# One load queue, other places for transposes and statistics, and a split last tile in an attention-and-GLU kernel

## The chip, the cores and the metric

The kernel runs on one core of one Trainium2 chip. The metric is the device time of one execution in microseconds (us). A profile of the same execution has a span, from the first to the last instruction, that is 1.7 to 1.8 us shorter than the timed figure. TensorE is PE in the profile (its weight loads PEld), VectorE is DVE, ScalarE is ACT, GpSimd is POOL, SyncE is SP.

## The reference, cut to what matters

```python
xn = _layernorm(x)                    # x: 2048 x 512, bf16
s  = _A_ref(xn, wqkv, wo)             # 32 heads of 16, each position looks at 8 places, 2 apart
g  = _silu(_B_ref(xn, w_gate, w_up, w_down))   # (gelu(xn w_gate) * (xn w_up)) w_down, inner width 1792
return x + s * g
```

## The kernel before

The 2048 rows are 16 tiles of 128, four tiles to a chunk of 512. For each tile VectorE computes mean and variance (`moments`), GpSimd turns the variance into a reciprocal root, VectorE normalizes, TensorE transposes and ScalarE copies the transposed tile out of PSUM. Then TensorE runs all projections. The parts that the change and the argument touch:

```python
    for t in range(TPQ):                                   # TPQ = 4
        load_x(t, queue=nc.scalar if t % 2 else nc.sync)   # 128 KB each
    for i in range(3):
        load_w(wqkv_sb, A_wqkv, i * D, (i + 1) * D)        # q, k, v thirds, 512 KB each
    load_x(TPQ, TPQ)                                       # tiles 4 to 7
    # [cut: the other weights and tiles, all on nc.sync]

    def moments(t):
        nc.vector.bn_stats(out=stats[:, t, :], in_=x_sb[:, t, :])
        nc.vector.bn_aggr(out=mv[:, t, :], in_=stats[:, t, :])
        nc.gpsimd.tensor_scalar(
            out=rstd[:, t, :], in0=mv[:, t, 1:2], scalar1=EPS, scalar2=None, op0=ALU.add
        )
        nc.gpsimd.tensor_tensor(out=rstd[:, t, :], in0=rstd[:, t, :], in1=mhalf[:], op=ALU.pow)

    # [cut] schedule of side work: at((stage, chunk, step), function, arguments)
    for i in range(TPQ):
        at(("qkv", 0, i), normalize, TPQ + i)
        at(("qkv", 0, 4 + i), moments, 2 * TPQ + i)
        at(("glu", 0, i), transpose, TPQ + i)
        at(("glu", 0, 8 + i), normalize, 2 * TPQ + i)
        at(("qkv", 1, 1 + 3 * i), transpose, 2 * TPQ + i)
        at(("glu", 0, 8 + i), moments, 3 * TPQ + i)

    # [cut] the start
    warm_up(10, TQ)                 # ten matmuls of 512 columns on zeros
    moments(0); moments(1); normalize(0); transpose(0); normalize(1)
    warm_up(2, P); transpose(1); warm_up(2, P)
    moments(2); moments(3); normalize(2); normalize(3)
    # [cut: moments of tiles 4 to 7]
    for hh in range(2):             # first for tiles 0, 1, then for tiles 2, 3
        for fo in range(2 * NC):    # eight groups (4 of q, 4 of k) of four 256-column matmuls
            qkv(0, fo, hh * HT * P, HT * P)
            if hh == 0 and fo in (4, 7):
                transpose(HT + fo // 6)       # tiles 2 and 3
```

The end of a tile is `down`: 14 matmuls into y, Silu on ScalarE (`sl`), four matmuls into s, then on VectorE m = s * sl and o_t = m + x, and a store of o_t.

The names in the profile: tr and xnT are a transposed tile before and after its copy out of PSUM (the memory that TensorE writes to), qkv_ps the projections, g_ps and u_ps the two products of the GLU (`ge` and `u` once ScalarE has them, h their product), pk the products of q and k, L_ps the logits, E their Exp, pv the products of E and v, o_ps the attention output. A step is the third number of the schedule and counts from 0.

The softmax here doesn't subtract the row's maximum and nothing guards it: scores larger than these inputs give would overflow.

Of the kernel before, what the change touches and what calls it, by code (L numbers as in the profile page):

```python
# [8 lines left out]
ALU = mybir.AluOpType  # L9
AF = mybir.ActivationFunctionType  # L10
BF16 = mybir.dt.bfloat16
F32 = mybir.dt.float32

P = 128
# [7 lines left out]
TQ = 512  # L22
# [6 lines left out]
def kernel(  # L29
# [13 lines left out]
    nc = tc.nc  # L43
    B, S, D = A_x.shape
    DF = B_w_gate.shape[1]
    NT, NC, NF, NJ = S // P, D // P, DF // P, S // TQ
    TPQ = TQ // P
    SV = PAD + S
    x2d, out2d = A_x[0], out[0]
# [3 lines left out]
    def pool(name, bufs, **kw):  # L53
        return ctx.enter_context(tc.tile_pool(name=name, bufs=bufs, **kw))
# [10 lines left out]
    op = pool("op", 1)  # L65
    sm = pool("sm", 3)
    sm2 = pool("sm2", 2)
    sm4 = pool("sm4", 4)
    dram = pool("dram", 1, space=bass.MemoryType.DRAM)
    mm = pool("mm", 5, space=bass.MemoryType.PSUM)  # L70
# [3 lines left out]
    x_sb = big.tile([P, NT, D], BF16, name="x_sb")  # L74
# [4 lines left out]
    wo_sb = wts.tile([P, NC, D], BF16, name="wo_sb")  # L79
    vT = dram.tile([D, SV], BF16, name="vT")  # L80

    def load_x(t, n=1, queue=nc.sync):
        queue.dma_start(
            out=x_sb[:, t : t + n, :],
            in_=x2d[t * P : (t + n) * P, :].rearrange("(t p) d -> p t d", p=P),
        )
# [4 lines left out]
        )  # L91

    for t in range(TPQ):
        load_x(t, queue=nc.scalar if t % 2 else nc.sync)
    for i in range(3):
        load_w(wqkv_sb, A_wqkv, i * D, (i + 1) * D)
    load_x(TPQ, TPQ)
    for i, (lo, hi) in enumerate(((0, DF // 2), (DF // 2, DF))):
        load_w(wg_sb, B_w_gate, lo, hi)
        load_w(wu_sb, B_w_up, lo, hi)  # L100
        load_x((2 + i) * TPQ, TPQ)

    def load_late_weights():
# [15 lines left out]
        out=vT.rearrange("(k p) n -> p k n", p=P)[:, :, 0:PAD],  # L119
        in_=warm[:, 0 : NC * PAD].rearrange("p (k n) -> p k n", k=NC),  # L120
# [48 lines left out]
    def moments(t):  # L169
        nc.vector.bn_stats(out=stats[:, t, :], in_=x_sb[:, t, :])  # L170
        nc.vector.bn_aggr(out=mv[:, t, :], in_=stats[:, t, :])
        nc.gpsimd.tensor_scalar(
            out=rstd[:, t, :], in0=mv[:, t, 1:2], scalar1=EPS, scalar2=None, op0=ALU.add
        )
        nc.gpsimd.tensor_tensor(out=rstd[:, t, :], in0=rstd[:, t, :], in1=mhalf[:], op=ALU.pow)  # L175
# [10 lines left out]
    def transpose(t):  # L186
        xn = xns[t]
        tr = mm.tile([P, NC * P], BF16, name="tr", tag="mm")
        for c in range(NC):
            nc.tensor.transpose(tr[:, c * P : (c + 1) * P], xn[:, c * P : (c + 1) * P], ident[:])  # L190
        j, i = divmod(t, TPQ)
        if i == 0:
            xnT[j] = xtp.tile([P, NC, TQ], BF16, name="xnT")
        nc.scalar.activation(  # L194
            out=xnT[j][:, :, i * P : (i + 1) * P],
            in_=tr[:].rearrange("p (c n) -> p c n", c=NC),
            func=AF.Copy,
        )

    def warm_up(n, cols):  # L200

        ps = mm.tile([P, TQ], F32, name="warm_ps", tag="mm")
        for _ in range(n):
            nc.tensor.matmul(
                ps[:, 0:cols], lhsT=warm[:, 0:P], rhs=warm[:, 0:cols], start=True, stop=True
            )
# [11 lines left out]
    st = [dict(pk={}, pv={}) for _ in range(NJ)]  # L218

    def qkv(j, fo, i0=0, n=TQ):  # L220
        which, c = divmod(fo, NC)
        if fo == 0 and i0 == 0:
            st[j]["q"] = qp.tile([P, NC, TQ], BF16, name="q_sb")
        ps = mm.tile([P, n], F32, name="qkv_ps", tag="mm")
        project(ps, wqkv_sb, fo * P, j, i0, n)
        if which == 0:
            nc.scalar.activation(out=st[j]["q"][:, c, i0 : i0 + n], in_=ps[:], func=AF.Copy)  # L227
        elif which == 1:
            lo = PAD + j * TQ + i0
            nc.scalar.activation(out=k_sb[:, c, lo : lo + n], in_=ps[:], func=AF.Copy)  # L230
        else:
            vst = sm4.tile([P, TQ], BF16, name="vst")
            nc.scalar.activation(out=vst[:], in_=ps[:], func=AF.Copy)  # L233
            lo = PAD + j * TQ
            nc.sync.dma_start(out=vT[c * P : (c + 1) * P, lo : lo + TQ], in_=vst[:])
# [121 lines left out]
    def down(j, tt):  # L357
        y = mm.tile([P, D], F32, name="y_ps", tag="mm")
        for fc in range(NF):
            nc.tensor.matmul(  # L360
                y[:],
                lhsT=st[j][fc][:, tt * P : (tt + 1) * P],
                rhs=wd_sb[:, fc, :],
                start=(fc == 0),
                stop=(fc == NF - 1),
            )
        sl = sm2.tile([P, D], BF16, name="sl")
        nc.scalar.activation(out=sl[:], in_=y[:], func=AF.Silu)  # L368
        s = mm.tile([P, D], F32, name="s_ps", tag="mm")
        for g in range(NC):  # L370
            nc.tensor.matmul(  # L371
                s[:],
                lhsT=st[j]["oT"][:, g, tt * P : (tt + 1) * P],
                rhs=wo_sb[:, g, :],
                start=(g == 0),
                stop=(g == NC - 1),
            )
        t = j * TPQ + tt
        m = sm2.tile([P, D], BF16, name="m")
        nc.vector.tensor_tensor(out=m[:], in0=s[:], in1=sl[:], op=ALU.mult)  # L380
        o_t = sm4.tile([P, D], BF16, name="o_t")
        nc.vector.tensor_tensor(out=o_t[:], in0=m[:], in1=x_sb[:, t, :], op=ALU.add)
        nc.sync.dma_start(out=out2d[t * P : (t + 1) * P, :], in_=o_t[:])


    side = {}
# [1 line left out]
    def at(key, fn, *args):  # L388
        side.setdefault(key, []).append((fn, args))
# [4 lines left out]

    for i in range(TPQ):
        at(("qkv", 0, i), normalize, TPQ + i)
        at(("qkv", 0, 4 + i), moments, 2 * TPQ + i)
        at(("glu", 0, i), transpose, TPQ + i)
        at(("glu", 0, 8 + i), normalize, 2 * TPQ + i)
        at(("qkv", 1, 1 + 3 * i), transpose, 2 * TPQ + i)  # L400
        at(("glu", 0, 8 + i), moments, 3 * TPQ + i)
        at(("qkv", 2, 2 * i), normalize, 3 * TPQ + i)
        at(("qkv", 2, 3 + 2 * i), transpose, 3 * TPQ + i)

# [28 lines left out]


    HT = TPQ // 2
    warm_up(10, TQ)
    moments(0)
    moments(1)
    normalize(0)
# [12 lines left out]
    for hh in range(2):  # L452
        for fo in range(2 * NC):
            qkv(0, fo, hh * HT * P, HT * P)
            if hh == 0 and fo in (4, 7):
                transpose(HT + fo // 6)
    for i in range(NC):
        run("qkv", 0, i)
        run("qkv", 0, NC + i)
# [3 lines left out]
    for j in range(NJ):  # L463
        for fc in range(NF):
            run("glu", j, fc)
            glu(j, fc)
        if j + 1 < NJ:
            for i in range(12):
                run("qkv", j + 1, i)
                qkv(j + 1, i)  # L470
        for tt in range(TPQ):
            run("down", j, tt)
            down(j, tt)
# [28 lines left out]
```

## Time and profile before

| | before |
|---|---|
| timed, first three runs | 236.25 us (236.22 to 236.42) |
| span of the profiled run | 234.4 us |
| first projection starts | 7.54 us |
| second half of the first projections starts | 12.38 us |
| last matmuls (s_ps) start | 229.31 us |

Timeline lines read: start in us, duration in us, engine, line, operation, output<-inputs, shapes, count; in brackets, how long the engine had been idle and what released it. Lines of a group of matmuls start at the first and end at the last one. The main readings are in the prediction. Two lines of the timeline of the kernel before are added here, because the argument comes back to them: the wait of VectorE for the first x tile, and a ScalarE operation in step 8 of the first GLU.

```profile
3.20 0.69 DVE L170 BATCH_NORM_STATS2 stats<-x_sb 128x6 f32<-128x512 bf16 x1 [1.97 <-DMA x_sb<-in_A_x_dram]
...
36.32 0.60 ACT L352 ACTIVATE u<-u_ps 128x512 bf16<-128x512 f32 x1 [0.63 <-PE u_ps L210]
```

The first says that tile 0 is there at 3.2 us. The second looked harmless when I predicted: ScalarE was idle 0.63 us before it; its neighbours of the same kind wait 0.33. The chain of waits of before has no engine to blame for the difference:

```profile
35.97 0.35 issue
36.32 0.60 ACT u L352
```

"Issue" is time in which the engine waited for nothing that the profile shows. From there to 50.28 this chain runs through ScalarE and VectorE, not through TensorE.

### The profile page before, as it was taken

To read this page: it belongs to the slowest core of one execution; us is meant where nothing else is said; L and a number is where in the kernel's file an instruction comes from. 1 tells how busy PE (TensorE), PEld (TensorE's weight loads), DVE (VectorE), ACT (ScalarE), POOL (GpSimd) and SP (SyncE) were. 2 spreads that over 40 slices of the span, in tenths; PEclk is the share of its full clock that TensorE was granted. 3 is DMA by queue.
4 is the path that set the end of the run, shared out by engine and by line. 5 is a ranking of instruction groups with operands and counts; after the bars stand their busy time and mean duration, and the time that the engine had idled before them with its cause. 6 is when DMAs were issued, how large, how long until landed. Compare 5 with 4: busy or idle time off the path is not lost.

```text
span 234.4 us, 3517 instructions
## 1 busy us (share of the span) xinstructions
PE 226.7 (97%) x1342; PEld 105.2 (45%) x1342; DVE 143.5 (61%) x214; ACT 135.8 (58%) x222; POOL 26.3 (11%) x80
## 2 busy tenths in 40 slices
PE   6889999999999999999999999999999999999993
PEld 2665444444444444445444444444444444444441
DVE  4458994896795288832559139961349529864131
ACT  2778868868512875757821397556641387576211
POOL 3268943400000000000000000000000000000000
PEclk9999999999999999999999999999999999999998
DMA  5999399820287300000266700000047810000001
GB/s 172 366 373 359 89 214 212 266 69 25 68 201 170 84 0 0 3 0 0 69 141 175 164 0 4 0 0 3 22 120 174 194 35 0 0 3 1 22 23 45
DMA packets 21793, 22.66 MB, mean 97 GB/s; under 512 B 1552, under 2 KB 21776, under 8 KB 21776
## 3 DMA queue, kind: packets, MB, share of 16 engines
q1 hardware_dynamic: 21488, 22.17, 35.5%
q10 hardware_dynamic: 288, 0.26, 0.3%
q8 instruction: 10, 0.16, 0.3%
q14 instruction: 7, 0.06, 0.1%
HBM read 18.22 MB, written 4.21 MB: 96 GB/s over the span
## 4 chain that ended last, share of the span: by engine, by line
PE 89%; DVE 4%; ACT 3%; issue 1%; DMA 1%; POOL 1%; DVEq 0%; ACTq 0%
PE y_ps L360 21%; PE g_ps L210 19%; PE u_ps L210 19%; PE qkv_ps L210 17%; PE s_ps L371 6%; PE o_ps L325 3%; PE L_ps L265 2%; DVE pv L311 2%; PE tr L190 1%; DMA x_sb<-in_A_x_dram 1%; ACT ge L350 1%; DVE stats L170 1%; ACT u L352 1%; DVE h L354 1%; POOL rstd L175 1%
## 5 line engine op out<-in xcount | busy, mean ns | idle before, releaser
L210 PE MATMUL g_ps<-xnT,wg_sb 128*128 128x512 bf16 x224 | 57.6, 379 | 0.0
L210 PE MATMUL u_ps<-xnT,wu_sb 128*128 128x512 bf16 x224 | 57.5, 379 | 0.0
L360 PE MATMUL y_ps<-wd_sb,h 128*128 128x512 bf16 x224 | 51.0, 379 | 0.0
L354 DVE TENSOR_TENSOR h<-ge,u 128x512 bf16<-128x512 bf16 x56 | 23.6, 422 | 36.3 <-ACT u L352 36.2
L210 PE MATMUL qkv_ps<-xnT,wqkv_sb 128*128 128x512 bf16 (+1 forms) x224 | 44.1, 349 | 1.3 <-ACT xnT L194 1.3
L255 DVE TENSOR_TENSOR pk<-q_sb,k_sb 128x2048 bf16<-128x2048 bf16 x32 | 37.8, 1220 | 12.2 <-ACT k_sb L230 12.2
L350 ACT ACTIVATE ge<-g_ps 128x512 bf16<-128x512 f32 x56 | 33.7, 601 | 14.2 <-PE g_ps L210 14.1
L352 ACT ACTIVATE u<-u_ps 128x512 bf16<-128x512 f32 x56 | 33.6, 600 | 14.2 <-PE u_ps L210 14.2
L311 DVE TENSOR_TENSOR pv<-E,v_arr 128x2048 bf16<-128x2048 bf16 x32 | 38.6, 1217 | 0.0
L368 ACT ACTIVATE sl<-y_ps 128x512 bf16<-128x512 f32 x16 | 9.6, 597 | 43.9 <-PE y_ps L360 43.9
L210 PEld LDWEIGHTS <-wu_sb 128*128 128x128 bf16 x224 | 21.9, 98 | 26.6 <-issue 0.3
L360 PEld LDWEIGHTS <-h 128*128 128x128 bf16 x224 | 21.9, 98 | 26.5
L210 PEld LDWEIGHTS <-wg_sb 128*128 128x128 bf16 x224 | 20.8, 98 | 26.6 <-issue 4.2
L210 PEld LDWEIGHTS <-wqkv_sb 128*128 128x128 bf16 x224 | 21.4, 98 | 19.1 <-issue 1.5
L380 DVE TENSOR_TENSOR m<-s_ps,sl 128x512 bf16<-128x512 f32 x16 | 11.0, 689 | 27.1 <-PE s_ps L371 27.1
L371 PE MATMUL s_ps<-wo_sb,oT 128*128 128x512 bf16 x64 | 16.4, 379 | 0.0
L170 DVE BATCH_NORM_STATS2 stats<-x_sb 128x6 f32<-128x512 bf16 x16 | 10.9, 680 | 7.1 <-DMA x_sb<-in_A_x_dram 7.1
L227 ACT ACTIVATE q_sb<-qkv_ps 128x512 bf16<-128x512 f32 (+1 forms) x20 | 10.2, 512 | 5.7 <-PE qkv_ps L210 5.3
L233 ACT ACTIVATE vst<-qkv_ps 128x512 bf16<-128x512 f32 x16 | 9.6, 597 | 5.0 <-PE qkv_ps L210 5.0
L194 ACT ACTIVATE xnT<-tr 128x512 bf16<-128x512 bf16 x16 | 9.5, 597 | 3.3 <-PE tr L190 3.3
L230 ACT ACTIVATE k_sb<-qkv_ps 128x512 bf16<-128x512 f32 (+1 forms) x20 | 10.2, 512 | 2.2 <-PE qkv_ps L210 1.9
L337 DVE TENSOR_TENSOR oT<-o_ps,rb 128x1024 bf16<-128x1024 f32 x8 | 9.8, 1219 | 2.0 <-PE o_ps L325 2.0
(42 smaller groups left out, 121.3 us busy)
## 6 DMA issues: line engine op xcount, KB each, us to landing
v_arr<-vT SPq DMA_DIRECT2D x16, 520.0 KB, 5.1
vT<-vst SPq DMA_DIRECT2D x16, 128.0 KB, 1.7
out_dram<-o_t SPq DMA_DIRECT2D x16, 128.0 KB, 2.5
wg_sb<-in_B_w_gate_dram SPq DMA_DIRECT2D x2, 896.0 KB
wu_sb<-in_B_w_up_dram SPq DMA_DIRECT2D x2, 896.0 KB, 13.0
wd_sb<-in_B_w_down_dram SPq DMA_DIRECT2D x1, 1792.0 KB, 17.2
wqkv_sb<-in_A_wqkv_dram SPq DMA_DIRECT2D x3, 512.0 KB, 6.7
x_sb<-in_A_x_dram SPq DMA_DIRECT2D x3, 512.0 KB, 10.4
```

Source lines behind the costliest of these rows:

```text
L170: nc.vector.bn_stats(out=stats[:, t, :], in_=x_sb[:, t, :])
L210: nc.tensor.matmul(ps[:], lhsT=w[:, dk, lo : lo + P], rhs=xnT[j][:, dk, i0 : i0 + n], start=(dk == 0), stop=(dk == NC - 1),)
L227: nc.scalar.activation(out=st[j]["q"][:, c, i0 : i0 + n], in_=ps[:], func=AF.Copy)
L230: nc.scalar.activation(out=k_sb[:, c, lo : lo + n], in_=ps[:], func=AF.Copy)
L255: nc.vector.tensor_tensor(out=pk[:], in0=st[j]["q"][:], in1=k_sb[:, :, off : off + TQ], op=ALU.mult)
L311: nc.vector.tensor_tensor(out=pv[:], in0=st[j]["E"][:, wh, :].unsqueeze(1).to_broadcast([P, 4, TQ]), in1=st[j]["va"][:, 4 * g : 4 * g + 4, ...
L350: nc.scalar.activation(out=ge[:], in_=g_ps[:], func=AF.Gelu_apprx_tanh)
L352: nc.scalar.activation(out=u[:], in_=u_ps[:], func=AF.Copy)
L354: nc.vector.tensor_tensor(out=h[:], in0=ge[:], in1=u[:], op=ALU.mult)
L360: nc.tensor.matmul(y[:], lhsT=st[j][fc][:, tt * P : (tt + 1) * P], rhs=wd_sb[:, fc, :], start=(fc == 0), stop=(fc == NF - 1),)
L371: nc.tensor.matmul(s[:], lhsT=st[j]["oT"][:, g, tt * P : (tt + 1) * P], rhs=wo_sb[:, g, :], start=(g == 0), stop=(g == NC - 1),)
L380: nc.vector.tensor_tensor(out=m[:], in0=s[:], in1=sl[:], op=ALU.mult)
```

## The change

The intent is to start TensorE's real work sooner, to close the hole in front of the second half of the first projections, to spread VectorE's statistics, and to shorten the end. The core of the diff (unchanged lines and the bodies of `load_x` and `down` cut):

```diff
     for t in range(TPQ):
-        load_x(t, queue=nc.scalar if t % 2 else nc.sync)
+        load_x(t)                                  # all on nc.sync
@@ moments
-        nc.gpsimd.tensor_scalar(
+        nc.vector.tensor_scalar(                   # variance + eps
@@ down
+        pieces = 2 if t == NT - 1 else 1           # last tile: s, m, o_t, store in two column halves
+            (nc.scalar if i else nc.sync).dma_start(
@@ schedule
-        at(("qkv", 0, 4 + i), moments, 2 * TPQ + i)
+        at(("glu", 0, 7 + i), moments, 2 * TPQ + i)
-        at(("glu", 0, 8 + i), moments, 3 * TPQ + i)
+        at(("glu", 1, 10 + i), moments, 3 * TPQ + i)
@@ start
-    warm_up(10, TQ)
+    warm_up(9, TQ)
-            if hh == 0 and fo in (4, 7):
-                transpose(HT + fo // 6)
+            if hh == 0 and fo in (2, 4):
+                transpose(HT + fo // 2 - 1)
```

More of the change, by code (lines that the diff above doesn't have):

```diff
@@ L80, with load_x @@
     vT = dram.tile([D, SV], BF16, name="vT")
-    def load_x(t, n=1, queue=nc.sync):
-        queue.dma_start(
+    def load_x(t, n=1):
+        nc.sync.dma_start(
             out=x_sb[:, t : t + n, :],
@@ L368, in down @@
         nc.scalar.activation(out=sl[:], in_=y[:], func=AF.Silu)
-        s = mm.tile([P, D], F32, name="s_ps", tag="mm")
-        for g in range(NC):
-            nc.tensor.matmul(
-                s[:],
-                lhsT=st[j]["oT"][:, g, tt * P : (tt + 1) * P],
-                rhs=wo_sb[:, g, :],
-                start=(g == 0),
-                stop=(g == NC - 1),
-            )
-        t = j * TPQ + tt
-        m = sm2.tile([P, D], BF16, name="m")
-        nc.vector.tensor_tensor(out=m[:], in0=s[:], in1=sl[:], op=ALU.mult)
-        o_t = sm4.tile([P, D], BF16, name="o_t")
-        nc.vector.tensor_tensor(out=o_t[:], in0=m[:], in1=x_sb[:, t, :], op=ALU.add)
-        nc.sync.dma_start(out=out2d[t * P : (t + 1) * P, :], in_=o_t[:])
+        t = j * TPQ + tt
+        o_t = sm4.tile([P, D], BF16, name="o_t")
+        pieces = 2 if t == NT - 1 else 1
+        n = D // pieces
+        for i in range(pieces):
+            cols = slice(i * n, (i + 1) * n)
+            s = mm.tile([P, n], F32, name="s_ps", tag="mm")
+            for g in range(NC):
+                nc.tensor.matmul(
+                    s[:],
+                    lhsT=st[j]["oT"][:, g, tt * P : (tt + 1) * P],
+                    rhs=wo_sb[:, g, cols],
+                    start=(g == 0),
+                    stop=(g == NC - 1),
+                )
+            m = sm2.tile([P, n], BF16, name="m")
+            nc.vector.tensor_tensor(out=m[:], in0=s[:], in1=sl[:, cols], op=ALU.mult)
+            nc.vector.tensor_tensor(out=o_t[:, cols], in0=m[:], in1=x_sb[:, t, cols], op=ALU.add)
+            (nc.scalar if i else nc.sync).dma_start(
+                out=out2d[t * P : (t + 1) * P, cols], in_=o_t[:, cols]
+            )
     side = {}
```

## The prediction

> **What bounds the kernel now.** I read the page's engine line first, then the chain of work that ended last, then the timeline of the first 13 us and of the last 5 us, because the diff edits mostly those two ends. The engine line of the page:
>
> ```profile
> PE 226.7 (97%) x1342; PEld 105.2 (45%) x1342; DVE 143.5 (61%) x214; ACT 135.8 (58%) x222; POOL 26.3 (11%) x80
> ```
>
> TensorE (PE) is busy 97% of the 234.4 us span; the other engines have slack. So only time in which TensorE stands still can be won. The chain of waits, first 20 us (start us, us, what), shows where that is:
>
> ```profile
> 0.79 2.39 DMA x_sb<-in_A_x_dram
> 3.20 0.70 DVE stats L170
> ...
> 5.36 0.61 POOL rstd L175
> 5.99 0.42 DVE xn L181
> 6.46 0.41 PE tr L190 x4
> 6.89 0.60 ACT xnT L194
> 7.54 2.35 PE qkv_ps L210 x20
> 10.11 1.32 PE qkv_ps L210 x12
> 11.46 0.38 ACT k_sb L230
> 11.84 0.50 ACT xnT L194
> 12.38 7.11 PE qkv_ps L210 x48
> ```
>
> Two holes are to be seen: the start-up chain of tiles 0 and 1 until the projections begin at 7.54, and a wait for the transposed tile 3 just before 12.38. From 12.38 the chain is nearly all PE until 230.36. The list of waits adds that the first hole is held from two sides:
>
> ```profile
> PE qkv_ps L210 <- ACT xnT L194: 1.3, 2, 0.7
> PEld L210 <- DMA wqkv_sb<-in_A_wqkv_dram: 0.6, 1, 0.6
> ```
>
> TensorE waited 1.3 us in two pieces for xnT (0.57 before 7.54 and 0.74 before 12.38 in the timeline), but the weight load also waited 0.6 us for the first third of wqkv, and started at 7.43. Activations and weights thus arrive within 0.1 us of each other. The third place is a DVE-paced wait in the first transition to chunk 1 (same view, later window):
>
> ```profile
> 47.96 2.28 DVE pv L311 x2
> 50.28 0.40 PE o_ps L325 x4
> ```
>
> The 16 matmuls of the first o_ps ran from 49.37 to the next group at 50.62, 1.25 us; the undisturbed o_ps groups of the same chain take 0.86 to 0.98. So 0.27 to 0.39 us are lost to late pv products. The timeline of the end:
>
> ```profile
> 229.31 1.03 PE L371 MATMUL s_ps<-wo_sb,oT 128*128 128x512 bf16 x4
> 229.51 0.60 ACT L368 ACTIVATE sl<-y_ps 128x512 bf16<-128x512 f32 x1 [3.29 <-PE y_ps L360]
> 230.45 0.69 DVE L380 TENSOR_TENSOR m<-s_ps,sl 128x512 bf16<-128x512 f32 x1 [2.73 <-PE s_ps L371]
> 231.17 0.42 DVE L382 TENSOR_TENSOR o_t<-m,x_sb 128x512 bf16<-128x512 bf16 x1
> 231.62 0.33 SPq L383 DMA_DIRECT2D out_dram<-o_t  x1
> ```
>
> After the last matmul come two DVE operations and a store that takes 2.8 us from its issue to the end of the span (234.4 - 231.6).
>
> **What the Trainium skill says.** "DMA: Bandwidth & Descriptors", section Issuing engines are not separate DMA queues: transfers from several issuing engines interleave on the same 16 engines, and a second issuer only saves the sequencer's time to issue. The trace agrees: two x tiles took 0.85 us to issue on SP and two 0.89 us on ACT, side by side, so one queue alone should need about 1.7 us for four. "TensorE: Matmul & The Clock Gate", Part 1: the array runs at half clock until about one window of 3.4 us of activity and falls back after an idle window. The trace agrees with the rise: weight loads of the warm-up follow each other at 0.42 us (1.65, 2.07, 2.50, ...) and from 4.17 closer; no fall is seen in gaps of 0.6 us. "VectorE: DVE Perf Modes", section on the TRN2 errata: each DVE operation carries a fixed cost. The trace agrees: PSUM-source operations take 0.689 us at 512 columns and 1.219 at 1024, so about 0.16 us fixed and 1.035 ns per column; bf16 from SBUF 0.424 at 512 and 1.22 at 2048, so again about 0.16 fixed and 0.52 ns per column.
>
> **The change part by part.**
>
> *x tiles on one queue.* Tile 0 no longer shares the engines with tile 1. It needed 2.39 us from issue to landing; the same 128 KB took 1.7 us in the quiet vT stores. I estimate 2.0, so the chain starts about 0.4 us earlier (2.8 instead of 3.2). The price: the issue of wqkv starts near 0.79 + 1.7 = 2.5 instead of 1.69. Its data, however, could not flow before the four x tiles (524 KB) were moved, and by the windows of the trace about 490 KB had moved by 3.5. An issue led to data some 1.1 us later (0.79 to about 1.9), so an issue at 2.5 gives data from 3.6. I therefore expect wqkv to land about when it did, 7.4 to 7.6, with a tail up to 8.2 if the 0.8 us of issue is paid in full.
>
> *eps on VectorE.* The GpSimd add lasts 0.22 us, the new DVE add about 0.12 to 0.16 (fixed cost), and one engine hop vanishes. But in tile 1's chain the DVE now does two adds in series: stats, mv, add, stats, mv, add, then the power on GpSimd. With x landing at T: stats T+0.02, mv +0.73, add +0.94, stats +1.02, mv +1.73, add +1.94, power +2.15, normalize +2.75, transpose +3.22, xnT +3.65, projection about +4.3. Before it was 7.54 - 3.18 = 4.36. So this part alone is worth 0.05 us; together with the earlier x the activations would allow a start near 7.1. The weights do not. The first projection starts at about **7.5**: gain 0.04 us, of which the weights eat 0.4.
>
> *One warm-up matmul fewer.* It is needed so that the transpose, now near 5.2, isn't behind the warm-up, which ended at 4.98. Worth nothing by itself.
>
> *Transposes of tiles 2, 3 after the third and fifth groups instead of the fifth and eighth.* The 32 projection matmuls and two transposes of the first half take 2.35 + 0.22 + 1.32 + 0.22 = 4.11 us. Tile 3's transpose comes after 5 groups (5 x 0.47) and one transpose, at 7.5 + 2.35 + 0.22 = 10.1; its copy on ScalarE, queued behind about one 0.4 us eviction, ends near 11.2. The second half starts at 7.5 + 4.11 = 11.6. The hole of **0.74** us closes (12.38 - 7.54 - 4.11 = 0.73). The normalized tiles are ready: in before 8.63 and 9.50, and needed at 8.9 and 10.1.
>
> *Moments of chunks 2 and 3 later.* Each is 0.69 + 0.18 us plus the new add, about 1.0 us of DVE. In the stretch of stages 8 to 11 of the first GLU one set stays, the first of them moves to stage 7 where DVE idled 0.17 us per stage. Behind stage 10 of chunk 0 the DVE runs without a gap from 41.68 to 51, so one statistics pair less (0.35 us net of the waits for u) brings the pv products forward by about 0.3 us and removes most of the o_ps wait: **0.26 us**. The logits at 35.85 need the eighth pk only for their second half, near 36.8, and I put it at 35.7. Chunk 3's set lands in stages 10 to 13 of the second GLU, where DVE idled 0.65, 1.30, 1.25 and 1.30 us before each h: hidden.
>
> *Last tile in two halves.* From the fits, m costs 0.16 + 256 x 1.035 ns = 0.42 us and o_t 0.29. Half 0 of s is done near 229.9, but m also needs sl, which ends at 230.11. So the DVE starts 0.3 us earlier, and then needs 2 x (0.42 + 0.29) = 1.42 instead of 1.13: the end stays at about 231.6. What is left is that the last store is 64 KB rather than 128: the windows show its data moving from about 232.4 to 232.95, so half saves about **0.2** us.
>
> Sum: 0.04 + 0.73 + 0.26 + 0.20 = 1.23 us, 236.25 - 1.2 = **235.05 us**.
>
> **The rivals.** (1) *The weights become the wait.* For it: the weight load waited until 7.43 already, and wqkv is now issued 0.8 us later. If it lands 0.8 us later, the start is 8.2 and the sum falls to 0.5: 235.75. Against it: the engines were busy with x anyway. (2) *The weights come earlier*, since the queue is clean and the dip of the rate to 150 GB/s between 3.7 and 4.5 us might vanish. Then the start is 7.1 and the time 234.65. (3) *The clock falls back.* TensorE now idles longer before the projections, from about 6.3 to 7.5, with fewer warm-up matmuls. One cold window would double the 256-column matmuls (0.117 us) for about 3.4 us and cost 1.7 us: 236.8. I give it one in twelve; the old gaps were nearly as long. (4) *VectorE becomes the bound* in stages 7 to 11, holding logits or pv: against it stand the 3.17 us it idled before 41.68. It would cost at most 0.5 us. (5) *The tail halves cost more than they save*, through an extra store on the ACT queue: within 0.2 us either way.
>
> **Range and chances.** Rivals 1 and 2 give 235.75 and 234.65, so 234.4 to 235.9 should hold eight times in ten. Two per cent is 4.7 us; all that TensorE stands still before its first projection and after its last matmul is 7.5 + 4.0 us, mostly untouched, so faster by 2% gets 0.01, slower 0.01, the same 0.98.
>
> **What would show it.** Right if: stats start near 2.8; the first projection waits for DMA wqkv near 7.5, not for xnT; no wait on xnT stands before the second half of the projections; the first o_ps of chunk 0 takes about 0.95 us; the last o_t still ends 1.2 us after the last s matmul, and the store's end follows by 2.6. Wrong if the first projection is past 8, if its matmuls run at 0.2 us, or if stats don't move.

## The result, and the profile after

The changed kernel took 234.61 us (234.44 to 234.72, 6 runs), the kernel before in the same rounds 236.43 us (236.22 to 236.56, 6 runs). A ratio here is the mean time of one kernel's fast runs over that of the other's of the same rounds, so it isn't quite the ratio of the medians; it is 0.9924 (95% interval 0.9911 to 0.9937). By medians the change gained 1.82 us; the prediction had 235.05 us, a gain of 1.2, and its range of 234.4 to 235.9 held.

The profiled span fell from 234.4 to 233.0, by 1.48 us before rounding (234.44 and 232.96). The engine line and the chain of waits of the changed kernel, first 20 us (start us, us, what):

```profile
PE 227.3 (98%) x1345; PEld 106.0 (46%) x1345; DVE 146.4 (63%) x232; ACT 135.6 (58%) x222; POOL 23.4 (10%) x64
...
0.80 2.04 DMA x_sb<-in_A_x_dram
2.86 0.70 DVE stats L170
...
6.20 0.62 PE tr L190 x4
6.84 0.61 ACT xnT L194
7.49 1.47 PE qkv_ps L210 x12
...
10.28 8.26 PE qkv_ps L210 x60
```

Against the same view of before: x lands at 2.84 instead of 3.18, but the first projection starts at 7.49, hardly sooner than 7.54. The hole is gone: from 10.28 on, 60 projection matmuls follow each other without a piece of ACT between them. The list of waits says the same; of the 1.3 us for xnT 0.5 is left, and the weight load still waited for its transfer:

```profile
PEld L210 <- DMA wqkv_sb<-in_A_wqkv_dram: 0.6, 1, 0.6
PE qkv_ps L210 <- ACT xnT L194: 0.5, 1, 0.5
```

One sign that the prediction gave was a first projection that waits for the weights and not for xnT. It came by half: the weight load waited for its transfer, and TensorE itself for xnT.

The chain line of the first o_ps group and the timeline of the end:

```profile
48.59 0.86 PE o_ps L325 x16
```

```profile
228.28 0.60 ACT L368 ACTIVATE sl<-y_ps 128x512 bf16<-128x512 f32 x1 [3.29 <-PE y_ps L360]
228.91 0.42 DVE L385 TENSOR_TENSOR m<-s_ps,sl 128x256 bf16<-128x256 f32 x1 [2.43 <-ACT sl L368]
...
230.03 0.29 DVE L386 TENSOR_TENSOR o_t<-m,x_sb 128x256 bf16<-128x256 bf16 x1
230.36 0.37 ACTq L387 DMA_DIRECT2D out_dram<-o_t  x1
```

The o_ps group runs in 0.86 us, without the split that the chain of before showed. At the end m now waits for sl (ScalarE) instead of s, as worked out; the halves last 0.42 and 0.29 us, as the fits said. The whole bookkeeping of the two spans:

| stretch | before | after | gain |
|---|---|---|---|
| to the first projection | 7.54 | 7.49 | 0.05 |
| from there to the first g_ps of the chain (19.71; 18.76) | 12.17 | 11.27 | 0.90 |
| from there to the last s matmuls (229.31; 228.08) | 209.60 | 209.32 | 0.28 |
| from there to the end (234.44; 232.96) | 5.13 | 4.88 | 0.25 |
| sum | | | 1.48 |

The second row is more than the 0.74 us of the hole. The 48 matmuls behind the hole took 7.11 us in before. In the changed kernel the same 48 are part of the 60 that took 8.26; less twelve at 0.11 us that leaves 6.94. In an unbroken stream a matmul starts before the one in front of it has ended (in before at 9.95, while the transpose ends at 10.11; ends are modelled), so a wait costs TensorE about 0.16 us more than its idle time. I call this the refill; the prediction left it out.

What the spans leave open is that the timed gain is 1.82, 0.3 more than their difference (the expectations below say 1.4 and 0.4, from the rounded spans). The profiled run of before (236.18 us) was quicker than all six timed ones (236.22 and up).

### The profile page after: what moved, and what is told of

It is laid out like the page before. It is cut to its first block, busy times and chain, and to the rows that moved or that the text cites. A ratio compares the mean times of both kernels' runs of the same rounds, so it can differ in the third digit from the quotient of the medians.

```text
span 233.0 us, 3523 instructions
## 1 busy us (share of the span) xinstructions
PE 227.3 (98%) x1345; PEld 106.0 (46%) x1345; DVE 146.4 (63%) x232; ACT 135.6 (58%) x222; POOL 23.4 (10%) x64
## 4 chain that ended last, share of the span: by engine, by line
PE 95%; DVE 2%; DMA 1%; ACT 1%; issue 0%
PE g_ps L210 21%; PE u_ps L210 21%; PE y_ps L360 21%; PE qkv_ps L210 18%; PE s_ps L377 6%; PE o_ps L325 3%; PE L_ps L265 3%; PE tr L190 2%; DMA x_sb<-in_A_x_dram 1%; DVE stats L170 1%; PE den_ps L285 0%; PE sp_ps L300 0%; DVE m L385 0%; ACT xnT L194 0%; ACT sl L368 0%; DVE o_t L386 0%
## 5 line engine op out<-in xcount | busy, mean ns | idle before, releaser
L385 DVE TENSOR_TENSOR m<-s_ps,sl 128x512 bf16<-128x512 f32 (+1 forms) x17 | 11.2, 658 | 26.8 <-PE s_ps L377 24.4
L175 POOL TENSOR_TENSOR rstd<-rstd,mhalf 128x1 f32<-128x1 f32 x16 | 10.4, 652 | 79.1 <-DVE rstd L172 79.1
L377 PE MATMUL s_ps<-wo_sb,oT 128*128 128x512 bf16 (+1 forms) x68 | 16.4, 366 | 0.0
```

What stands on the lines that cost most here:

```text
L377: nc.tensor.matmul(s[:], lhsT=st[j]["oT"][:, g, tt * P : (tt + 1) * P], rhs=wo_sb[:, g, cols], start=(g == 0), stop=(g == NC - 1),)
L385: nc.vector.tensor_tensor(out=m[:], in0=s[:], in1=sl[:, cols], op=ALU.mult)
```

## The experiments

Each experiment ran in a round with the kernel before. "Cost" is the rise of (median minus the median of before in the same rounds) against the changed kernel, whose figure is -1.82, or against the one with ten warm-up matmuls, whose figure is -1.91. The three groups of experiments ran on different chips, but their medians of before agree with each other and with the result's (236.43, 236.54, 236.49, 236.49). Runs that lost the clock (see u6 and n2 below) count as fast and are in medians and ratios; without them no cost changes by more than 0.05 us, except that of u4.

### u1: transposes of tiles 2 and 3 back

```diff
-            if hh == 0 and fo in (2, 4):
-                transpose(HT + fo // 2 - 1)
+            if hh == 0 and fo in (4, 7):
+                transpose(HT + fo // 6)
```

> The changed kernel with the transposes of tiles 2 and 3 put back behind the fifth and eighth group. My theory: the hole before the second half of the projections (0.74 us) comes back, and with it the refill of the pipeline behind it (0.15 us), so this one part is worth 0.9 us: a time about 0.9 us above the changed kernel, and a wait of some 0.7 us for xnT just before the second half. Rival: the hole was only moved in time and TensorE catches up later, or the wait is on something else (xn of tile 3, ScalarE's queue); then less than 0.4 us.

Measured: 235.62 us (235.50 to 237.19) against 236.54, cost 0.90 us. In the chain of waits the projections start at 7.42, the copy of tile 3 stands in front of the second half, and that half again takes 7.11 us:

```profile
11.71 0.50 ACT xnT L194
...
12.26 7.11 PE qkv_ps L210 x48
```

It is as the theory has it, the refill included. One of six runs took 237.19 at a mean clock of 0.993; more of that below.

### u2 and w1: moments of chunks 2 and 3 back

```diff
-        at(("glu", 0, 7 + i), moments, 2 * TPQ + i)
+        at(("qkv", 0, 4 + i), moments, 2 * TPQ + i)
-        at(("glu", 1, 10 + i), moments, 3 * TPQ + i)
+        at(("glu", 0, 8 + i), moments, 3 * TPQ + i)
```

> The changed kernel with the moments of chunks 2 and 3 at their old places. My theory: the only thing that comes back is the late pv products before the first o_ps group, 0.28 us. Rival: the moments' removal from the early VectorE queue matters more (pk products or normalized tiles of chunk 1 that TensorE or ScalarE waits for), then 0.5 us or more; or nothing, if the o_ps wait went away for the eps add.

Measured: 235.55 us (235.18 to 236.79) against 236.54, cost 0.83 us, three times what I expected; the profiled run was the one of 236.79. I repeated it with ten warm-up matmuls:

> The changed kernel with ten warm-up matmuls (no falls of the clock in its four runs) and the moments of chunks 2 and 3 at their old places. Theory: late pv products alone, 0.3 to 0.5 us over the 234.58 of ten warm-ups with the moments moved. Rival: the 0.8 to 0.9 us that the same step cost at nine warm-ups, not by the clock but by a further wait of VectorE or TensorE that this trace would show.

Measured: 235.30 us (234.94 to 236.00) against 236.49, cost 0.72 us. The timeline of that run shows two waits that the same kernel with the moments moved doesn't have:

```profile
19.05 0.69 DVE L170 BATCH_NORM_STATS2 stats<-x_sb 128x6 f32<-128x512 bf16 x1 [3.12 <-DMA x_sb<-in_A_x_dram]
...
20.54 0.40 PE L190 MATMUL tr<-ident,xn 128*128 128x128 bf16 x4 [0.18 <-DVE xn L181]
...
49.68 0.40 PE L325 MATMUL o_ps<-pv,hsum 128*32 128x512 bf16 x4 [0.21 <-DVE pv L311]
```

The transpose of tile 5 in the kernel with the moments moved (u6):

```profile
20.18 0.39 PE L190 MATMUL tr<-ident,xn 128*128 128x128 bf16 x4
```

VectorE works its queue in order. It stood 3.12 us in front of the statistics of tile 8, which arrives only at 19 us, and the normalization of tile 5, whose data had long been there, stood behind. TensorE reached the transpose of tile 5 and had to wait: it started at 20.54, where the kernel with moved moments has it at 20.18, so 0.36 us went there. The late pv products then cost 0.39 (the next group starts 1.36 us after the first o_ps matmul instead of 0.97). In the kernel before this cost TensorE nothing: its transpose of tile 5 came 1.1 us later (21.27), and tile 8 was there 0.8 us sooner (its statistics start at 18.25). So the rival was right: the move of the moments is worth more once the head is faster. The o_ps wait is in the trace of u2 too (again 1.36 us). The wait at tile 5 is in that of w1 alone: in u2 TensorE, late by the fallen clock, finds the tile there, and the statistics of tile 8 start at 18.42. How often a run pays those 0.36 us isn't shown.

### u3: last tile in one piece

```diff
-        pieces = 2 if t == NT - 1 else 1
+        pieces = 1
```

> The changed kernel with the last tile finished in one piece. My theory: the last o_t ends at the same distance from the start of the last s matmuls as in halves (2.2 to 2.3 us), and only the larger last store costs 0.2 us. Rival: the second store queue costs as much as it saves, no difference within 0.05 us.

Measured: 234.81 us (234.78 to 234.84) against 236.54, cost 0.09 us. The last matmuls start at 227.98 and the span ends at 233.08, 5.10 us later, against 4.88 in the changed kernel. The ends give 0.22 us, the medians 0.09; I take 0.1 to 0.2.

### u4 and w2: x tiles on two queues again

```diff
-        load_x(t)
+        load_x(t, queue=nc.scalar if t % 2 else nc.sync)
```

> The changed kernel with the x tiles on two queues again. My theory: x lands 0.3 to 0.4 us later, the activations then arrive with or after the weights, and the first projection starts 0.0 to 0.3 us later than 7.49. Rival, from the 0.4 us by which the timed gain of the whole change (1.8) is above the gain in the profiled spans (1.4): using ACT's queue at the start costs time that the span doesn't show; then the time rises by 0.4 us with the span's start of projections unchanged.

Measured: 236.85 us (235.36 to 238.65) against 236.54: worse than before, cost 2.13 us, with a wide spread. Two things are mixed. The clock is one, and its part is below: three of the six runs lost it (0.984 to 0.993). Two more took 236.66 and 236.72 at a clock of 1.000, against 235.36 for the quickest; no trace of them was kept, and what they lost stays open. With ten warm-up matmuls it is steadier:

> The changed kernel with ten warm-up matmuls and the x tiles on two queues. Theory: tile 0 lands 0.3 to 0.6 us later, so does the first projection, and the o_ps wait comes back by the later ScalarE u (0.25 us): 0.5 to 0.9 us over 234.58; a longer gap for TensorE, so some runs still lose the clock (1.3 us more), fewer than with nine. Rival: the ten warm-ups hide all of it, under 0.3 us.

Measured: 235.46 us (235.35 to 236.09) against 236.49, cost 0.88 us. Lines of the timeline of that run:

```profile
3.64 0.69 DVE L170 BATCH_NORM_STATS2 stats<-x_sb 128x6 f32<-128x512 bf16 x1 [2.41 <-DMA x_sb<-in_A_x_dram]
...
8.06 1.47 PE L210 MATMUL qkv_ps<-xnT,wqkv_sb 128*128 128x256 bf16 x12 [0.57 <-ACT xnT L194]
...
35.95 0.60 ACT L352 ACTIVATE u<-u_ps 128x512 bf16<-128x512 f32 x1 [0.64 <-PE u_ps L210]
```

Tile 0 arrives at 3.64 instead of 2.93 in the ten-matmul kernel with one queue, and the first projection starts at 8.06 instead of 7.35. The rest is the last line: ScalarE's u of step 8 waits 0.64 us instead of 0.33, the softmax's Exp, behind it in ScalarE's queue, is late by as much, and the first o_ps group takes 1.20 us to the next group instead of 0.97.

### b1: the kernel before once more

No edit.

> The kernel before, unchanged, for a second trace. The timed gain of the change is 1.8 us, the gain between the two profiled spans 1.4; the profiled run of before (236.18) lies 0.3 us under the median of its other runs. Theory: in a typical run the two queues let tile 0 land later than in that trace (3.4 to 3.6 us instead of 3.18), and the first projection starts 0.2 to 0.4 us after 7.54. Rival: tile 0 lands at 3.2 again and the 0.3 us lie elsewhere (half clock at the start, or behind the first projections).

Measured: 236.43 us, span 234.7. Lines of its timeline:

```profile
3.44 0.69 DVE L170 BATCH_NORM_STATS2 stats<-x_sb 128x6 f32<-128x512 bf16 x1 [2.22 <-DMA x_sb<-in_A_x_dram]
...
7.79 2.34 PE L210 MATMUL qkv_ps<-xnT,wqkv_sb 128*128 128x256 bf16 x20 [0.57 <-ACT xnT L194]
```

Tile 0 landed 0.24 us later than in the profile I predicted from, and the first projection started 0.25 later. The spans of the other undisturbed runs of before in these rounds are 234.6 to 235.2, so this trace is the typical one. Against it the changed kernel starts its projections 0.3 us sooner, not 0.05.

### p2: only the x tiles on one queue, the rest as before

The edit is the first hunk of the diff alone.

> The kernel before with only the x tiles put on one queue. Theory from the experiment that undid this part: tile 0 lands at 2.9 to 3.0 and the first projection starts at 7.3 to 7.5; by itself it gains 0.2 to 0.5 us over the kernel before, and the later start of ScalarE's u in stage 8 (0.3 us, seen in both traces with x tiles on ScalarE's queue) is gone. Rival of the prediction: the weights arrive with the issue delay and hold the first projection, gain under 0.1 us.

Measured: 235.70 us (235.61 to 237.75) against 236.49, a gain of 0.79 us (ratio 0.995, interval 0.9899 to 1.0002, wide because runs with a fallen clock are in both means; without these the medians are 235.70 and 236.44, a gain of 0.74). Lines of its timeline:

```profile
7.31 2.34 PE L210 MATMUL qkv_ps<-xnT,wqkv_sb 128*128 128x256 bf16 x20 [0.57 <-ACT xnT L194]
...
35.78 0.60 ACT L352 ACTIVATE u<-u_ps 128x512 bf16<-128x512 f32 x1 [0.33 <-PE u_ps L210]
...
49.13 1.04 PE L325 MATMUL o_ps<-pv,hsum 128*32 128x512 bf16 x16
```

The start is 0.48 us sooner than in the typical trace of before, and the o_ps wait is gone although no statistics were moved: ScalarE's u is in time again. So the wait that I had put down to VectorE's statistics was, in the kernel before, settled by the late u. The four traces with x tiles on ScalarE's queue (before, b1, u4, w2) have the late u (0.63 to 0.65), all the others have 0.33. What delays it isn't shown ("issue" in the chain of before); the instruction lists of ScalarE differ by the two load instructions at their start, and I leave it open.

### u5: eps on GpSimd again

```diff
-        nc.vector.tensor_scalar(
+        nc.gpsimd.tensor_scalar(
```

> The changed kernel with eps added on GpSimd again. My theory (the working of the prediction): tile 1's chain is the same within 0.1 us, so a time within 0.1 us of the changed kernel's (234.5 to 234.8 at the earlier chip's scale). Rival: the GpSimd add in front of each power delays tile 1 by the 0.2 us that it lasts, and the first projection starts 0.2 us later; or tile 0's earlier transpose changes what TensorE's clock does.

Measured: 234.81 us (234.66 to 235.06) against 236.49, cost 0.14 us. The first projection starts at 7.47, as expected; but it waited for the weights there, so this start doesn't show what eps does to the chain of tile 1. The copy of tile 1 (xnT) does: it starts 3.70 us after the first statistics here and 3.77 in u6, so with the add on VectorE the chain is 0.07 us longer. The cost is elsewhere. First the line of this run, then its counterpart in the changed kernel:

```profile
43.38 0.41 DVE L181 TENSOR_SCALAR xn<-x_sb,mv,rstd 128x512 bf16<-128x512 bf16 x1 [0.77 <-POOL rstd L175]
```

```profile
42.96 0.41 DVE L181 TENSOR_SCALAR xn<-x_sb,mv,rstd 128x512 bf16<-128x512 bf16 x1 [0.44 <-POOL rstd L175]
```

At their new place the moments of a tile stand only one step in front of its normalization, so VectorE waits for GpSimd's round trip. With the add on GpSimd that wait is 0.77 us, with it on VectorE 0.44, and the pv products follow. The part that I had called worth 0.05 us for the head is worth its 0.14 because of where the moments went.

### n1: first third of the weights ahead of tiles 2 and 3

```diff
-    for t in range(TPQ):
-        load_x(t)
-    for i in range(3):
+    load_x(0); load_x(1); load_w(wqkv_sb, A_wqkv, 0, D)
+    load_x(2); load_x(3)
+    for i in range(1, 3):
         load_w(wqkv_sb, A_wqkv, i * D, (i + 1) * D)
```

> The changed kernel with the first third of wqkv issued behind tiles 0 and 1 and ahead of tiles 2 and 3. Theory of the prediction (the weights hold the first projection): it lands up to 0.5 us earlier, the first projection then waits for xnT alone and starts at 7.2 to 7.4 instead of 7.4 to 7.6; gain 0.1 to 0.2 us. Rival: the activations hold it already (in two of the four traces so far the weights were there first); no gain, and tiles 2 and 3 come later, which may cost up to 0.3 us at their transposes.

Measured: 234.97 us (234.60 to 235.52) against 236.49, 0.30 us worse than the changed kernel. Its profiled run (234.60, the quickest of five) started the projections at 7.36, waiting for xnT and not for the weights; what the slower runs lost, it doesn't show. So weights that come sooner don't help: the rival was right. In the traces with one queue the start lies between 7.31 and 7.61, and the last thing to come was xnT in u1, u3, u6, n1, n2, p2 and w1, the weights in u2 and u5 (by the lists of waits); in the changed kernel they were 0.1 us apart.

### u6 and n2: the clock

u6 has ten warm-up matmuls, n2 has nine and 4 and 8 small ones instead of 2 and 2 behind the two first transposes.

> The changed kernel with ten warm-up matmuls. In two traces (moments undone, x queues undone) the granted clock fell to half for one window of 3.41 us just as the projections began, after a window in which TensorE was busy 1.73 and 1.76 us; in the kernel before 1.88 us were enough to keep it. Theory: the tenth matmul adds 0.2 us (full clock) to that window, so no run falls back, and the median is that of the changed kernel or up to 0.1 us more where the warm-up holds tile 0's transpose back (half clock, end at 5.5). Rival: the fall has to do with the start of the projections alone; then falls (runs 1.3 us or more above the median, clock 0.993) come as often as in the changed kernel's head so far, 2 in 17.

> The changed kernel with eight more small filler matmuls (4 and 8 instead of 2 and 2) behind the transposes of tiles 0 and 1. Theory: TensorE's busy time in the window before the projections rises by 0.43 us (full clock) to about 2.15, above the 1.88 that kept the clock and the 1.75 that lost it, so no run falls back: spread of the runs under 0.4 us, median as the changed kernel's. Rival: the fillers only delay the second transpose or the first projection, the median rises by 0.2 us or more.

The ground for both lies in the runs of u2 and u4. The view of stretches has, after the start and end, the length, then busy time and count of PE, PEld, DVE, ACT and POOL, then the granted clock, DMA share and GB/s. First three stretches of the profiled run of u2, then one of the kernel before:

```profile
0.59:4.00 3.41, 2.75 (x7) 1.04 (x8) 1.19 (x5) 1.28 (x1) 0.54 (x3) 1.00 0.54 155
4.00:7.41 3.41, 1.73 (x15) 0.77 (x13) 2.83 (x10) 1.18 (x2) 1.20 (x2) 1.00 0.92 280
7.41:10.83 3.42, 3.22 (x18) 2.42 (x19) 1.60 (x5) 1.17 (x5) 1.19 (x2) 0.50 1.10 353
```

```profile
4.12:7.53 3.41, 1.88 (x16) 0.97 (x15) 2.67 (x7) 1.19 (x2) 1.81 (x5) 1.00 0.94 301
```

The clock goes in windows of 3.41 us. In u2 TensorE was busy 1.73 us of the window in front of the projections, and the next window was granted half the clock, so the first dozen or so projection matmuls ran at half speed. In u4 the same happened after 1.49 us (4.47 to 7.88; the record of the clock has half speed from 7.88 to 11.29. The 1.76 and 1.75 in the two expectations come from a window that I had set 0.28 us too early). In before 1.88 us were enough, and in the other eleven traces the window that follows the rise of the clock had 1.94 to 3.03 and kept it. (The 1.00 of the first stretch isn't to be trusted: the warm-up matmuls in it follow each other at 0.42 us, half speed. The record only starts when the clock is first raised.) A run that loses the clock takes 1.2 to 2.3 us more than the median of its kernel (u4 apart, where half of the runs lost it).

Measured: u6 234.58 us (234.52 to 234.64, 4 runs), n2 234.66 us (234.59 to 234.86, 5 runs), against 236.49; no fall in either, and with w1 and w2 none in 21 runs. But it isn't settled by the warm-up count. The kernel before, with ten, lost the clock in 5 of its 37 runs (238.2 to 238.8 us, clock 0.993) and p2, with ten, in 1 of 6; the kernels with the changed head and nine lost it in 2 of 33 (all the runs of the changed kernel, u1, u2, u3, u5 and n1; none of the six of the changed kernel itself); u4, with nine and a start at 8.0, lost it in 3 of 6. Where the windows fall differs from run to run, and these numbers are too small for a rate. u6 is the fastest kernel by 0.09 us, inside the differences between rounds.

## Why the prediction was right or wrong

**Transposes: right, a little small.** 0.73 was said, 0.90 measured in the spans and by u1. The term left out is the refill, 0.16 us.

**x on one queue: the step that was mis-sized.** The prediction has x landing near 2.8 (2.84) and the projections at about 7.5 (7.49), "gain 0.04 us". The start in that trace is right; what it is to be compared with was not. The profiled run of before was a quick one; a typical one starts at 7.79 (b1). And the queue change does a second thing that no step had: it brings ScalarE's u, the Exp and the pv products forward. By itself it is worth 0.79 us (p2). Of the 0.6 us between the predicted 1.2 and the timed 1.82, the typical start explains 0.25 and the refill 0.16; the rest I can't split by these runs.

**"The weights do not": wrong as a cause.** In the profile of the changed kernel the weights came at 7.4 as predicted, but n1 and p2 show that the activations alone allow no start before about 7.3. Rival 1, weights late by the full 0.8 us of issue, did not come: one queue starts at 7.31 to 7.61. Rival 2, 7.1, didn't either; the chain of tile 1, which was to take 4.3 us and allow a start near 7.1, is longer. From the first statistics it takes 7.49 - 2.86 = 4.63 us in the changed kernel, where the transposes ran at half clock (0.61 us instead of 0.40), and 7.35 - 2.93 = 4.42 in u6, where they did not.

**The o_ps wait: the number right by luck, the cause wrong.** 0.26 was said, 0.28 measured. The prediction read the chain from 12.38 on as nearly all TensorE; from 35.97 to 50.28 it is ScalarE, VectorE and issue, with the late u at its head. The step said that one statistics pair less on VectorE removes it. p2 removes it without that, and w2 brings it back with the statistics moved. With the whole change in place both are needed: the old order alone brings the o_ps wait back (1.36 us to the next group in w1) and costs 0.72 us, half of it at the transpose of tile 5, which was hidden before. Rival 4, VectorE as the bound, did not come in the changed kernel: no wait for pv is left.

**eps: wrong for the head, by 0.1 us, and worth its 0.14 us elsewhere.** It was to shorten the chain of tile 1 from 4.36 to 4.3 us. From the first statistics to the first projection, where xnT came last and the transposes had the full clock, the traces have 4.34 to 4.35 us with the add on GpSimd (before, b1, p2) and 4.42 to 4.43 with it on VectorE (u1, u3, u4, u6, n1, n2, w1, w2). The term that was too small is the power: from its start to the normalization of tile 1 it is 0.69 us (5.11 to 5.80 in u6), where the prediction had 0.60; with the add on GpSimd it is 0.62 (5.17 to 5.79 in u5). The gain is at the new place of the moments (0.14 us, u5).

**The tail: right.** VectorE ends 2.24 us after the start of the last s matmuls (before 2.28), and the smaller store saves the rest: 0.25 between the spans of before and after, 0.22 and 0.09 by u3's span and medians (0.2 said). Rival 5, halves that cost more than they save, did not come.

**The clock: rival 3 is real.** It was given one in twelve and 1.7 us. It took 2 of 33 runs with nine warm-up matmuls, and the kernel before has it as well, so it is no effect of the change that these runs could show.

The parts don't add up, and that is part of the answer. Undone one at a time they cost 0.90, 0.72, 0.88, 0.14 and 0.1 us, 2.7 in all, against 1.82 for the whole. x on one queue (0.79), the transposes (0.90) and the tail (0.1) make 1.8 without the other two, which keep VectorE out of the way of the faster head (0.72 and 0.14 us if undone). A kernel with just those three was not run, so whether moments and eps together gain anything over leaving both alone stays open.

## What to carry to other kernels

When one engine is 97% busy, look for the few places where it stands still and follow each back through the queues that are worked in order: an instruction that waits for late data holds up everything behind it, and that can stay hidden until another part gets faster. Take more than one profile of the kernel before you predict: here 0.25 us of the start-up came and went with the arrival of one tile. And a part's worth is what it is worth beside the others; undo each in the final kernel, and try the main one alone as well.

## What the Trainium skill lacked or had wrong

- "TensorE: Matmul & The Clock Gate", Part 1: its table gives an idle window of about 3.4 us as what drops the clock; how much of a window may be busy, the page doesn't say. Here windows with TensorE busy 1.73 and 1.49 of 3.41 us dropped it (u2, u4, transposes counted), and none with 1.88 or more did (twelve traces). Half busy was not enough. The window's length agrees: the fallen clock lasted 3.41 us.
- "TensorE: Matmul & The Clock Gate", Part 1: a busy window raises the clock; again without the share. 2.75 us of 3.41 did (u2), 2.44 did not (the changed kernel, 0.28 to 3.69). So the changed kernel's first transposes still ran at half clock at 6.2 us, five us after the warm-up began: where the windows lie decides, as the page says.
- "DMA: Bandwidth & Descriptors", section Issuing engines are not separate DMA queues: right that a second queue saves only issue time. It tells of the interleaving, but not of its price: the first of several tiles waits for its companions. Tile 0's statistics start at 2.86 to 3.05 us with one queue (ten traces) and 3.20 to 3.64 with two (four traces).
- No page I found has a reason for the late ScalarE operation: 0.63 to 0.65 us of idle time before u in step 8 in the four kernels that issue two loads from ScalarE's queue at the start, 0.33 in the others. The chain of before calls 0.35 us of it "issue".
